# A constant moved into padding columns, warm-up products on fp32 data, and a new issue order, in a gated-linear-attention plus MLP-mixer kernel

## The chip, the cores and the metric

One core of one Trainium2 chip runs the kernel. The metric is the device time of one execution in microseconds (us). Matrix products run on TensorE (PE in the profile, its weight loads PEld), elementwise work on VectorE (DVE), ScalarE (ACT) and GpSimd (POOL), and DMAs are issued from SyncE (SP) and ACT.

## The reference

Inputs q, k, v and alpha have the shape 4 x 8 x 768 x 48 (batch, heads, steps, head dimension), in float32. A recurrent attention runs over the 768 steps, and its output x (4 x 768 x 384) goes through a mixer of two small MLPs:

```python
state = zeros((B, H, D, D))
for t in range(S):
    state = alpha[:, :, t, :, None] * state + einsum('bhd,bhe->bhde', k[:, :, t], v[:, :, t])
    y[:, :, t] = einsum('bhd,bhde->bhe', q[:, :, t], state)
...
xt = x.transpose(0, 2, 1)
h = maximum(xt @ w_tok1, 0) @ w_tok2          # 768 -> 256 -> 768
u = x + h.transpose(0, 2, 1)
out = u + maximum(u @ w_ch1, 0) @ w_ch2       # 384 -> 1536 -> 384
```

## The kernel before

The steps of a batch are cut into three chunks of 256, so there are twelve chunks, 0 to 11. In a chunk a partition holds two neighbouring steps ("slots"), and the first 64 partitions are one half (128 steps), the last 64 the other. The recurrence is replaced by products: with c the running sum of log(alpha) inside a half, queries are scaled by exp(c), keys by exp(-c), and the output is a masked product of the two plus a term with the state at the start of the half.

Names of operations carry their chunk at the end. For chunk n, `ld_at`, `ld_kt`, `ld_qt`, `ld_vt` load alpha, k, q, v. `ln` (chunks 0 to 2, the "wide" ones) or `P`, `ln1`, `lnP`, `r1` (the others) take logarithms into the tile `la`, which has 64 columns a head, 48 of data and 16 of padding. `cumw` or `cum` forms the running sums c in PSUM by products with a triangular matrix, and behind them 16 columns of sums over each half, one pair a head. One of each pair must vanish in exp for the partitions of the other head; for that a product of the identity with a small constant tile `off` adds -1024 there. `E`, `Et` and `IE` are the exps of c, of the sums and of -c. `kk`, `kl`, `qq`, `ql` scale keys and queries (`k0a`, `q0r` prepare the first slot), `vb` casts v, `vs` swaps halves of it. `trk` and `trq` transpose on TensorE and `evk`, `evq` copy the result out of PSUM (chunks 6 to 11 use the DMA transposes `dk`, `dq` and a copy `pq`). `G` is the product of keys and queries, `mask` its masking, `K` the product for the state, `s`, `sa`, `sm` the state's update, `i` and `y` the two terms of the output, `x` its copy to bf16.

For a mixer of batch b, `t1` and `t2` are the products with w_tok1 and w_tok2, `ht` the relu between them, `u` the residual add, `up` and `ut` (batches 0 and 1) or the DMA transposes `ux` the turning of u, `c1` the product with w_ch1, `rt` its relu, `c2` the product with w_ch2, `o` the residual add and `st` the store. `ldw` loads a piece of weights, `cw` casts it.

`f1` and `f3` are fillers: one or three products of zeros into a bank that an operation is about to overwrite, for TensorE alone; nobody reads them.

Each engine runs its instructions in order. That order is written out: the string `ORDER` lists all operations, each with a letter for its engine (t TensorE, s ACT, v DVE, g POOL, y SP), and the string `BUFS` names the buffers in the order in which they are first needed. The order between engines is kept by waits on data and buffers alone, with one addition: operations of DVE and POOL that read and write SBUF only (`shared`) wait for the last such operation of the other engine.

Of the kernel before, what the change touches and what calls it, by code (L numbers as in the profile page):

```python
# [102 lines left out]
OFF = -1024.0  # L103
NS, NM, NDT, NDC = 6, 3, 2, 12
# [12 lines left out]
def build(g):  # L117
# [12 lines left out]
    def attention(n):  # L130
# [19 lines left out]
        if n in WIDE:  # L150
            lnp = O("ln", act(800, True), 0, writes=[la], reads=[at], preds=[ld["at"]], emit=lambda e: g.lnw(la, at))
            cb = V("pair")
            cum = O("cumw", pe([384] * 4 + [4] * 8 + [16]), 2, writes=[cb, E, IE], reads=[la], preds=[lnp] + fill("cumw", cb),
# [4 lines left out]
        else:  # L158
# [7 lines left out]
            cum = O("cum", pe([384] + [4] * 4 + [16]), 2, writes=[cb, E, IE], reads=[la], preds=[lnp] + fill("cumw", cb),  # L166
# [10 lines left out]
        def scale(names, dst, src, f, pre, raw):  # L177
            return [O(nm, either(dve(384 * len(sl)), pool_tt(384 * len(sl))), 5, writes=[dst], reads=[src, f], port=True,
                      preds=(pre if 0 in sl else raw) + ([e2] if f is IE else [e1]),
                      emit=lambda e, sl=sl: g.scaled(e, dst, src, f, wide, sl)) for nm, sl in zip(names, slots)]  # L180
# [198 lines left out]
kk1v ld_vt1y vb1v K1t sm1_0v sa0_1t trk1t E2s ld_qt2y Et2s sm0_1v vs1_0g y1_0t evk1s ql2v sa1_1t qq2v x1_0s ib1t  # L379
sm1_1v y0_0t vs0_1s x0_0s G0_1t trq2t mask0_1v ld_kt2y kl2g f1_G11t G1_1t mask1_1v ia1t y0_1t kk2g trk2t ld_vt2y vb2s  # L380
K2t sa0_2t ldw_wt10y vs1_1g y1_1t ldw_wt11y evk2v evq2s G0_2t x0_1s f3_G12t G1_2t cw_wt11s cw_wt10g t1_0_1_0t sm0_2v
ib2t ia2t mask0_2v t1_0_1_1t vs0_2s y0_2t t1_0_0_0t t1_0_0_1t t1_0_1_2t mask1_2v x1_1s vs1_2g y1_2t x0_2v ldw_wt20y
t1_0_0_2t t1_0_0_3t t1_0_1_3t t1_0_1_4t t1_0_0_4t x1_2s t1_0_0_5t t1_0_1_5t ht_0_1s ht_0_0v cw_wt20g t2_0_2t ld_at3y
P3g t2_0_0t ldw_wt21y cw_wt21g u_0_2v ld_at4y P4g u_0_0v t2_0_1t lnP3s ln13s cum3t u_0_1v t2_0_3t u_0_3v t2_0_4t ln14s
r14s t2_0_5t IE3s lnP4s up_0_0t ut_0_0s up_0_1t ldw_wc11y cum4t IE4s u_0_4v u_0_5v up_0_2t ut_0_2s E4s ut_0_1v
cw_wc11g E3s c1_0_2_0t ldw_wc13y ld_kt3y cw_wc13g c1_0_6_0t c1_0_3_0t k0a3v kl3v kk3v kb3g c1_0_6_1t c1_0_3_1t
rt_0_3_1v rt_0_2_0v ldw_wc12y cw_wc12s r13s c1_0_2_1t c1_0_7_1t rt_0_3_0v ldw_wc15y cw_wc15s c1_0_7_0t rt_0_7_0v trk3t
c1_0_4_1t rt_0_6_0s ldw_wc10y c1_0_11_0t ka3s ldw_wc14y cw_wc14g rt_0_2_1s cw_wc10s rt_0_6_1v rt_0_4_1v ld_qt3y
c1_0_5_1t evk3s q0r3v ql3v c1_0_8_1t rt_0_11_0s qq3v ld_vt3y vb3v vs0_3v kc3v rt_0_5_1s c1_0_0_1t c1_0_8_0t rt_0_0_1s
rt_0_7_1s rt_0_8_1s c1_0_9_0t c1_0_1_0t vs1_3v rt_0_1_0s trq3t c1_0_5_0t rt_0_9_0v evq3s rt_0_8_0s c1_0_1_1t K3t  # L390
# [12 lines left out]
ld_qt7y u_1_0v lnP8s ln18s t2_1_1t u_1_1v t2_1_5t u_1_5v up_1_1t r17s c2_0_3_2t up_1_0t c2_0_3_3t u_1_4v up_1_2t
ld_qt8y dk6y ut_1_1v E7s o_0_3v ut_1_2v ut_1_0s k0a7g P10g vs0_6s kk7v ld_kt9y dk7y cum8t IE8s k0a8g c1_1_5_0t dq6y
ld_qt9y c1_1_9_0t o_0_0v P9g c1_1_8_0t q0r7v qq7g c1_1_10_0t c1_1_6_1t vs1_6s rt_1_5_0s r18s c1_1_4_0t kb6s E8s
c1_1_1_0t c1_1_7_1t rt_1_1_0v ka6s rt_1_9_0v c1_1_1_1t rt_1_4_0s c1_1_8_1t vs1_7s rt_1_8_0v kc6g c1_1_2_0t c1_1_11_1t
rt_1_11_1v vs0_7g rt_1_6_1s dq7y rt_1_1_1s rt_1_8_1v c1_1_7_0t c1_1_0_0t q0r8v rt_1_7_0s c1_1_3_1t rt_1_7_1s
rt_1_10_0s ld_vt8y K6t rt_1_2_0v ka7s kc7s c1_1_4_1t s0_6v sa1_6v ld_vt9y kk8g sm1_6g c1_1_5_1t rt_1_5_1s c1_1_3_0t
rt_1_3_0v c1_1_11_0t lnP9s rt_1_0_0s rt_1_3_1v pq6g c1_1_9_1t rt_1_11_0s kb7s c1_1_10_1t rt_1_10_1s rt_1_4_1v
rt_1_9_1v cum9t c1_1_0_1t k0a9g K7t sa0_7v rt_1_0_1v E9s IE9s sm0_7g sa1_7v c1_1_2_1t rt_1_2_1s c2_1_1_0t G1_6t qq8g  # L410
G0_6t mask0_6v ld_qt10y c2_1_3_0t c2_1_3_1t c2_1_3_2t c2_1_3_3t c1_1_6_0t c2_1_1_1t c2_1_4_0t dk8y kk9v ln110s pq7s
ln19s r110s r19s q0r9g sm1_7g mask1_6v dq8y rt_1_6_0s dk9y c2_1_1_2t G1_7t G0_7t o_1_3v ld_kt10y ib7t ib6t y1_6t vb8s
vs1_8s mask1_7v c2_1_4_1t c2_1_4_2t y0_6t c2_1_4_3t mask0_7v vs0_8s o_1_4v c2_1_1_3t o_1_1v lnP10s x1_6s kc8s K8t qq9g
dq9y sa0_8v ka9s vb9s cum10t c2_1_0_0t E10s ld_kt11y x0_6v ia7t y0_7t IE10s pq8g G0_8t mask0_8v ld_at11y vs1_9s G1_8t
# [481 lines left out]
```

## Time and profile before

| what | value |
|---|---|
| time, median of 3 runs | 163.1 us (163.03 to 163.98) |
| the profiled execution | 162.81 us, span 161.1 us |
| TensorE busy | 154.0 us, 96% of the span |
| VectorE / ScalarE / GpSimd busy | 117.2 / 101.1 / 64.4 us |
| DMA | 34.46 MB, mean 214 GB/s |

The span reaches from the first to the last instruction that the profiler saw; the execution's own time has 1.7 us more around it. In the rows, a line number is that of kernel.py, and as all products of the attention go through one helper, they share the line 607 and are told apart by their tiles: `ps<-zs` is a filler, `ps<-la,u` the running sums, `ps<-off,idn` the constant, `ps<-idn,pkk` a transpose of keys. A matmul's duration includes its way through the array, so neighbouring ones overlap, and x8 merges eight of them.

### The profile page before, as it was taken

The numbers are of one execution on the slowest core, as the hardware profiler recorded it, in microseconds if no ns is written. First come the engines' busy times: TensorE is split into PE (matmuls) and PEld (weight loads), VectorE is DVE, ScalarE is ACT, GpSimd is POOL, SyncE is SP. The second block draws the span as 40 slices with busy tenths as digits, with TensorE's granted clock in tenths as the row PEclk, the third lists the DMA queues.
The fourth block names the chain that finished last, engine by engine and source line by source line (L and its number), as shares of the span: only waits on it lengthen the run. The fifth ranks groups of instructions, "written<-read, shape, count | busy, mean of one in ns | idle before, by whom it ended". The sixth has DMA issues, their size and how long they took to land.

```text
span 161.1 us, 4038 instructions
## 1 busy us (share of the span) xinstructions
PE 154.0 (96%) x1598; PEld 98.7 (61%) x1598; DVE 117.2 (73%) x211; ACT 101.1 (63%) x190; POOL 64.4 (40%) x78
## 2 busy tenths in 40 slices
PE   7969898899999999999999999999999999999992
PEld 2556665666675666766666776666666566655661
DVE  4169796969899999858879999896696813654151
ACT  3794995999996867996999973889610002243000
POOL 4044396330915381976988994024320000000000
PEclk9987999999999999999999999999999999999999
DMA  4999999999999899999998999997110174331215
GB/s 121 323 325 311 296 336 347 353 283 271 293 368 285 202 300 288 316 224 265 235 250 168 190 304 173 166 263 212 54 49 4 26 169 146 140 108 49 98 58 187
DMA packets 76322, 34.46 MB, mean 214 GB/s; under 512 B 68112, under 2 KB 76304, under 8 KB 76304
## 3 DMA queue, kind: packets, MB, share of 16 engines
q1 hardware_dynamic: 74288, 31.66, 77.1%
q10 hardware_dynamic: 2016, 2.56, 4.4%
q8 instruction: 12, 0.20, 0.5%
q14 instruction: 6, 0.05, 0.1%
HBM read 25.17 MB, written 4.72 MB: 185 GB/s over the span
## 4 chain that ended last, share of the span: by engine, by line
PE 91%; ACT 5%; DVE 1%; issue 1%; DVEq 0%
PE ps L832 29%; PE ps L837 29%; PE ps L607 19%; PE ps L813 5%; PE ps L808 5%; PE ps L669 3%; ACT tpq L700 1%; ACT IE L640 1%; ACT E L640 1%; PE ps L824 1%; ACT tpk L700 1%; ACT ut L700 1%; DVE ht L805 0%; DVE ut L701 0%; ACT E L644 0%
## 5 line engine op out<-in xcount | busy, mean ns | idle before, releaser
L837 PE MATMUL ps<-wc,rt 128*128 128x384 bf16 (+2 forms) x300 | 52.4, 320 | 0.0
L832 PE MATMUL ps<-ut,wc 128*128 128x384 bf16 x288 | 50.9, 326 | 0.5 <-DVE ut L701 0.5
L803 ACT ACTIVATE rt<-ps 128x384 bf16<-128x384 f32 x56 | 26.1, 491 | 29.1 <-PE ps L832 26.1
L832 PEld LDWEIGHTS <-wc 128*128 128x128 bf16 x288 | 27.1, 98 | 17.5 <-issue 0.6
L837 PEld LDWEIGHTS <-rt 128*128 128x128 bf16 x300 | 27.4, 98 | 16.2
L723 DVE TENSOR_TENSOR gtm<-ps,mk 128x1024 bf16<-128x1024 f32 x24 | 28.7, 1218 | 2.6 <-PE ps L607 2.5
L805 DVE TENSOR_SCALAR rt<-ps 128x384 bf16<-128x384 f32 x40 | 20.6, 551 | 7.5 <-PE ps L832 7.4
L841 DVE TENSOR_TENSOR in<-ps,u 128x384 f32<-128x384 f32 (+2 forms) x25 | 13.1, 537 | 13.6 <-PE ps L837 13.2
L700 ACT CAST vb<-in 64x384 bf16<-64x384 f32 (+1 forms) x23 | 14.8, 649 | 2.1 <-DMA in<-in_v_dram 1.4
L656 POOL TENSOR_TENSOR pkq<-in,E 128x768 bf16<-128x768 f32 (+1 forms) x9 | 13.0, 1457 | 7.8 <-ACT IE L640 6.9
L817 DVE TENSOR_TENSOR u<-ps,x 128x384 bf16<-128x384 f32 x24 | 11.7, 550 | 1.3 <-PE ps L813 1.1
L774 POOL TENSOR_TENSOR ss<-tmp,E 128x384 bf16<-128x384 f32 x9 | 7.5, 836 | 7.8 <-DVE tmp L771 5.1
L656 POOL TENSOR_TENSOR pkk<-in,IE 128x384 bf16<-128x384 f32 (+1 forms) x6 | 8.4, 1409 | 5.4 <-ACT x L700 3.0
L808 PE MATMUL ps<-x,wt 128*128 128x384 bf16 x48 | 10.4, 325 | 0.0
L652 POOL TENSOR_TENSOR in<-in,lf 128x384 f32<-128x384 f32 x5 | 5.0, 1006 | 12.8 <-DVE rt L805 7.1
L592 POOL TENSOR_TENSOR in<-in 128x384 f32<-128x384 f32 x8 | 8.0, 1000 | 4.9 <-DVE pkk L656 3.7
L607 PE MATMUL ps<-tpq,tpk 48*64 48x128 bf16 (+1 forms) x288 | 8.6, 224 | 1.3 <-ACT E L644 0.9
L607 PE MATMUL ps<-zs 128*128 128x512 bf16 x25 | 8.5, 485 | 1.1 <-DVE zs L507 1.1
L813 PE MATMUL ps<-ht,wt 128*128 128x384 bf16 x48 | 8.6, 325 | 0.5 <-DVE ht L805 0.5
L700 ACT CAST x<-ps 128x384 bf16<-128x384 f32 x16 | 7.7, 481 | 2.2 <-PE ps L607 1.8
L607 PEld LDWEIGHTS <-tpk 48*64 48x64 bf16 (+1 forms) x288 | 6.1, 104 | 4.4 <-issue 2.6
L607 PE MATMUL ps<-vb,gtm 128*128 128x48 bf16 x192 | 8.7, 183 | 0.0
(93 smaller groups left out, 214.9 us busy)
## 6 DMA issues: line engine op xcount, KB each, us to landing
in<-in_alpha_dram SPq DMA_DIRECT2D x12, 384.0 KB, 5.3
in<-in_q_dram SPq DMA_DIRECT2D x12, 384.0 KB, 5.6
in<-in_k_dram SPq DMA_DIRECT2D x12, 384.0 KB, 5.0
in<-in_v_dram SPq DMA_DIRECT2D x12, 384.0 KB, 5.5
in<-in_moe_w_ch_dram SPq DMA_DIRECT2D x12, 384.0 KB, 6.2
out_dram<-in ACTq DMA_DIRECT2D x12, 192.0 KB, 2.0
out_dram<-in SPq DMA_DIRECT2D x11, 192.0 KB, 2.2
in<-in_moe_w_tok_dram SPq DMA_DIRECT2D x4, 384.0 KB, 5.7
```

The lines of the kernel that those rows point to most:

```text
L607: return self.pe.matmul(out, lhsT=lhsT, rhs=rhs, start=start, stop=stop, skip_group_check=True)
L656: self.shared(self.eng[e].tensor_tensor(self.t(dst)[:, c : c + z, :, 0:D], self.t(src)[:, :, c : c + z, :].rearrange("p h s d -> p s h d") ...
L700: return self.act.copy(d, s)
L723: self.nc.vector.tensor_tensor(self.t(gtm)[:, hf, :, :], self.pair(gp).rearrange("p a (j t) -> p (a j) t", t=128), bass.AP(tensor=m.tensor ...
L803: self.act.activation(d, s, AF.Relu)
L805: self.nc.vector.tensor_scalar_max(d, s, 0.0)
L808: self.pe.matmul(self.bank(bank)[:, 0:HD], lhsT=self.wt1[:, kc, m * 128 : m * 128 + 128], rhs=self.t(x), start=(kc == 0), stop=(kc == NS - 1))
L813: self.pe.matmul(self.bank(bank)[:, 0:HD], lhsT=self.wt2[:, kc, i * 128 : i * 128 + 128], rhs=self.t(hts[kc]), start=(kc == 0), stop=(kc = ...
L817: self.nc.vector.tensor_tensor(self.t(u)[:, i % 3], self.bank(bank)[:, 0:HD], self.t(x), ALU.add)
L832: self.pe.matmul(self.bank(bank)[:, 0:HD], lhsT=self.wc1[:, kc, mc * 128 : mc * 128 + 128], rhs=self.t(ut)[:, 3 * half : 3 * half + 3, kc, ...
L837: self.pe.matmul(self.bank(bank)[:, 0 : cz - ca], lhsT=self.t(rts[mc][0])[:, i * 128 : i * 128 + 128], rhs=self.wc2[:, mc, ca:cz], start=( ...
L841: self.nc.vector.tensor_tensor(self.row(o)[:, ca:cz], self.bank(bank)[:, 0 : cz - ca], self.t(u)[:, i % 3, ca:cz], ALU.add)
```

## The change

Three things are changed. The product with `off` is gone: -1024 stands in two padding columns of `la` (row 0 and row 64), and the running-sum product takes 50 columns a head in place of 48 and spreads it by the triangular matrix. So c and the sums lie together, 50 columns a head, in PSUM and (chunks 3 to 11) in the tile `E`, and what reads them takes that step. The fillers become one product each, on zeros read as fp32, of 384 columns for `f3` and 128 for `f1`, where they were three and one of 512 in bf16. And `ORDER` and `BUFS` are new as a whole; the set of operations is the same. Some stay on their engine and move in the order, some change the engine.

```diff
-        self.off = T([128, 16], BF16, "off")
-        self.zs = T([128, 128], BF16, "zs")
+        self.zs = T([128, 256], BF16, "zs")
...
-        off = self.off.rearrange("p (c r) -> p c r", r=2)
-        dv.memset(self.off, 0.0)
-        dv.memset(off[0:64, :, 1:2], OFF)
-        dv.memset(off[64:128, :, 0:1], OFF)
+        for t in self.T["la"]:
+            dv.memset(t[0:1, 0, :, D + 1 : D + 2], OFF)
+            dv.memset(t[64:65, 0, :, D : D + 1], OFF)
...
     def fill(self, bank, count):
-        for _ in range(count):
-            z = self.zs
-            z = bass.AP(tensor=z.tensor, offset=z.offset, ap=[list(z.ap[0]), [0, 4], [1, 128]])
-            self.mm(self.bank(bank), self.zs, z, True, True)
+        z, n = self.zs.bitcast(F32), 384 if count > 1 else 128
+        r = bass.AP(tensor=z.tensor, offset=z.offset, ap=[list(z.ap[0]), [0, n // 128], [1, 128]])
+        self.mm(self.bank(bank)[:, 0:n], z, r, True, True)
+
+    def heads(self, bank, w=D):
+        return bank[:, 0 : H * DT2].rearrange("p (h c) -> p h c", c=DT2)[:, :, 0:w]
+
+    def sums(self, b, a, slots):
+        t = b[:, 0 : H * DT2].rearrange("p (h c) -> p h c", c=DT2)
+        for j in range(4):
+            for sl in slots:
+                self.mm(t[:, 2 * j : 2 * j + 2, D:DT2], a[:, sl, 2 * j : 2 * j + 2, :], self.sel, False,
+                        j == 3 and sl == slots[-1])
...
     def cumw(self, cb, la):
         b0, b1, a = self.bank(cb, 0), self.bank(cb, 1), self.t(la)
-        self.mm(b1[:, 0:HD], self.u2, a[:, 0, :, 0:D], True, False)
-        self.mm(b1[:, 0:HD], self.u2, a[:, 1, :, 0:D], False, True)
-        self.mm(b0[:, 0:HD], self.u2, a[:, 0, :, 0:D], True, False)
-        self.mm(b0[:, 0:HD], self.us, a[:, 1, :, 0:D], False, True)
-        ...
-        self.mm(b1[:, HD : HD + 16], self.idn, self.off, False, True)
+        self.mm(b1[:, 0 : H * DT2], self.u2, a[:, 0, :, 0:DT2], True, False)
+        self.mm(self.heads(b1), self.u2, a[:, 1, :, 0:D], False, False)
+        self.mm(self.heads(b0), self.u2, a[:, 0, :, 0:D], True, False)
+        self.mm(self.heads(b0), self.us, a[:, 1, :, 0:D], False, True)
+        self.sums(b1, a, (0, 1))
```

The start of the new order, with the engines' letters (loads of SP in their own order are at0 at1 kt0 vt0 at2 qt0 qt1 kt1 qt2 vt1 kt2 vt2 wt10 wt11 wt20 at4 wt21 at3 wc10 wc11 wc13 wc12 wc14 kt3 qt3; before they were at0 at1 qt0 kt0 qt1 vt0 at2 kt1 vt1 qt2 kt2 vt2 wt10 wt11 wt20 at3 wt21 at4 wc11 wc13 kt3 ...):

```diff
-f1_trq0t f3_cumw0t ld_at0y ln0s ld_at1y f1_K0t f3_K0t f3_cumw1t f3_trq0t ln1s cumw0t Et0s f3_trk0t E0s ld_qt0y qq0v
-ql0v ld_kt0y cumw1t IE0s kl0v trq0t E1s IE1s kk0v ld_qt1y ql1g evq0s trk0t evk0v qq1g Et1s G0_0t mask0_0v G1_0t
-ld_vt0y vb0s K0t s0_0v f3_trq1t vs0_0g f1_trq1t trq1t ld_at2y ln2s evq1s sa1_0t ib0t mask1_0v ld_kt1y kl1g cumw2t IE2s
...
+f1_trq1t f3_cumw1t f3_K0t ld_at0y ln0s f3_trk0t ld_at1y ln1s f3_cumw0t cumw0t IE0s cumw1t E1s IE1s Et1s Et0s ld_kt0y
+f1_K0t ld_vt0y kl0v kk0v trk0t vb0v K0t vs1_0g s0_0v ld_at2y ln2s cumw2t evk0v ld_qt0y E0s qq0v ql0v IE2s ld_qt1y qq1v
+ql1v E2s f1_trq0t f3_trq0t trq0t evq0s Et2s sa1_0t sm1_0v f3_trq1t trq1t G0_0t evq1s ld_kt1y kl1v kk1v ld_qt2y ql2g
+qq2g trk1t evk1s ld_vt1y mask0_0v G1_0t mask1_0v vs0_0g f1_G11t G1_1t mask1_1v G0_1t vb1s ib0t y1_0t x1_0s K1t vs1_1s
+vs0_1s ld_kt2y kk2v sa0_1t sm0_1v ld_vt2y y0_0t x0_0s trq2t ia1t mask0_1v sa1_1t kl2g ib1t y1_1t trk2t evq2s x1_1s
+y0_1t x0_1s vb2g K2t vs0_2s sm1_1v sa0_2t ia2t evk2v G0_2t ... f3_G12t G1_2t ...
...
```

Later places that the prediction names, in the new order: the first products of batch 0's channel MLP with chunk 3 among them (TensorE: `c1_0_0_0 c1_0_3_0 c1_0_2_0 c1_0_1_0 c1_0_6_0 c1_0_7_1 c1_0_7_0 c1_0_3_1 c1_0_5_0 c1_0_6_1 c1_0_0_1 c1_0_1_1 c1_0_4_1 trk3 c1_0_5_1 c1_0_9_0 c1_0_2_1 trq3`), where DVE has `rt_0_7_1 k0a3 kk3 kl3 q0r3` and POOL then `ql3 qq3` (DVE had `q0r3 ql3 qq3` before); and the end, where the last stores `st_3_0h0` and `st_3_0h1` are issued by SP (ACT before).

More of the change, by code (lines that the diff above doesn't have):

```diff
@@ L103 @@
 OFF = -1024.0
+DT2 = D + 2
 NS, NM, NDT, NDC = 6, 3, 2, 12
@@ L179, in scale @@
                       preds=(pre if 0 in sl else raw) + ([e2] if f is IE else [e1]),
-                      emit=lambda e, sl=sl: g.scaled(e, dst, src, f, wide, sl)) for nm, sl in zip(names, slots)]
+                      emit=lambda e, sl=sl: g.scaled(e, dst, src, f, wide, sl, DT2 if f is E and not wide else D))
+                    for nm, sl in zip(names, slots)]
         kk = scale(("kk", "kl"), pkk, kt, IE, k_in, [ld["kt"]])
@@ L620, in cum @@
-        self.mm(b[:, HD : HD + 16], self.idn, self.off, False, True)
+        self.mm(b[:, 0 : H * DT2], self.u2, a[:, 0, :, 0:DT2], True, False)
+        self.sums(b, a, (0,))
     def cumw(self, cb, la):
         b0, b1, a = self.bank(cb, 0), self.bank(cb, 1), self.t(la)
-        self.mm(b1[:, 0:HD], self.u2, a[:, 0, :, 0:D], True, False)
-        self.mm(b1[:, 0:HD], self.u2, a[:, 1, :, 0:D], False, True)
-        self.mm(b0[:, 0:HD], self.u2, a[:, 0, :, 0:D], True, False)
-        self.mm(b0[:, 0:HD], self.us, a[:, 1, :, 0:D], False, True)
@@ L633, in expE @@
+        self.sums(b1, a, (0, 1))
     def expE(self, E, cb):
[L634 removed]
+        self.act.activation(self.t(E)[:, 0 : H * DT2], self.bank(cb)[:, 0 : H * DT2], AF.Exp)
     def expIE(self, IE, cb):
[L637 removed]
+        self.act.activation(self.t(IE)[:, 0:HD].rearrange("p (h d) -> p h d", h=H), self.heads(self.bank(cb)), AF.Exp,
+                            scale=-1.0)
@@ L652, in q0r, with scaled @@
         self.shared(self.eng[e].tensor_tensor(a, a, self.t(r1), ALU.mult))
-    def scaled(self, e, dst, src, f, wide, slots):
+    def scaled(self, e, dst, src, f, wide, slots, step):
         f, c, z = self.t(f), slots[0], len(slots)
@@ L658, in scaled @@
             bass.AP(tensor=f.tensor, offset=f.offset + (c * HD if wide else 0),
-                    ap=[list(f.ap[0]), [HD if wide else 0, z], [D, H], [1, D]]), ALU.mult))
+                    ap=[list(f.ap[0]), [HD if wide else 0, z], [step, H], [1, D]]), ALU.mult))
     def vcast(self, e, vb, vt):
@@ L754, in amul @@
     def amul(self, E, hf, wide):
-        f = self.t(E)[:, (2 * HD if wide else HD) + 2 * hf :]
-        return bass.AP(tensor=f.tensor, offset=f.offset, ap=[list(f.ap[0]), [4, 4], [1, 2], [0, D]])
+        at, step = (2 * HD + 2 * hf, 2) if wide else (DT2 * hf + D, DT2)
+        f = self.t(E)[:, at:]
+        return bass.AP(tensor=f.tensor, offset=f.offset, ap=[list(f.ap[0]), [2 * step, 4], [1, 2], [0, D]])
     def st(self, t):
```

143 lines of the change are left out of this document (67 added, 76 removed), and 22 rows, old and new, of the table BUFS.

## The prediction, made before the changed kernel ran

> **What bounds the kernel now.** I read the page first, then TensorE's waits, then the start by the microsecond, because the page says that TensorE is hardly ever idle.
>
> ```profile
> span 161.1 us, 4038 instructions
> PE 154.0 (96%) x1598; PEld 98.7 (61%) x1598; DVE 117.2 (73%) x211; ACT 101.1 (63%) x190; POOL 64.4 (40%) x78
> PE 91%; ACT 5%; DVE 1%; issue 1%; DVEq 0%
> PE ps L607 <- DVE zs L507: 1.1, 1, 1.1
> PE ps L607 <- ACT E L644: 0.9, 1, 0.9
> ```
>
> The third line is the chain that ended last: 91% of it is TensorE. The last two are the longest waits of TensorE (total, times, longest), and both lie in the first 11 us. And behind the start? The two windows below (us, length, then busy time of PE, PEld, DVE, ACT, POOL) stand for 40 to 155 us.
>
> ```profile
> 40.00:50.00 10.00, 10.00 (x124) 6.73 (x123) 9.10 (x14) 9.57 (x19) 5.72 (x7) 1.00 1.07 331
> 140.00:150.00 10.00, 10.00 (x64) 6.07 (x63) 5.41 (x12) 3.81 (x8) 0.00 (x0) 1.00 0.28 99
> ```
>
> From the first hidden-layer product (c1, line 832) on, no gap is left, and 64 products in 10 us is one every 0.156 us. This stretch can lose by a new order, by waits, but can win only what is taken off TensorE. So a better order pays only ahead of that product. That start is worth a walk:
>
> ```profile
> 1.06 4.59 PE L607 MATMUL ps<-zs 128*128 128x512 bf16 x14 [1.06 <-DVE zs L507]
> 1.46 0.15 PEld L607 LDWEIGHTS <-zs 128*128 128x128 bf16 x1 [0.28 <-issue]
> 4.27 0.84 ACT L601 ACTIVATE la<-in 128x768 bf16<-128x768 f32 x1 [2.18 <-DMA in<-in_alpha_dram]
> 5.48 0.65 PE L607 MATMUL ps<-la,u 128*128 128x384 bf16 x3
> 6.34 0.17 PE L607 MATMUL ps<-off,idn 128*128 128x16 bf16 x1
> 6.31 0.10 PEld L607 LDWEIGHTS <-idn 128*128 128x128 bf16 x1
> 6.36 0.81 PE L607 MATMUL ps<-zs 128*128 128x512 bf16 x3
> 6.63 0.81 ACT L640 ACTIVATE E<-ps 128x768 f32<-128x768 f32 x1
> 11.79 0.84 ACT L601 ACTIVATE la<-in 128x768 bf16<-128x768 f32 x1 [0.25 <-DMA in<-in_alpha_dram]
> 12.43 1.87 PE L607 MATMUL ps<-zs 128*128 128x512 bf16 x4
> 14.79 1.31 ACT L700 COPY tpq<-ps 128x1024 bf16<-128x1024 bf16 x1 [2.16 <-PE ps L669]
> ...
> 18.58 0.40 PE L607 MATMUL ps<-tpq,tpk 48*128 48x128 bf16 x8 [0.38 <-ACT tpk L700]
> 22.61 2.37 DVE L723 TENSOR_TENSOR gtm<-ps,mk 128x1024 bf16<-128x1024 f32 x2
> 27.04 1.14 PE L813 MATMUL ps<-ht,wt 128*128 128x384 bf16 x6 [0.49 <-DVE ht L805]
> 27.56 2.88 DVE L817 TENSOR_TENSOR u<-ps,x 128x384 bf16<-128x384 f32 x6 [0.58 <-PE ps L813]
> 31.33 0.97 PE L832 MATMUL ps<-ut,wc 128*128 128x384 bf16 x5 [0.49 <-DVE ut L701]
> ```
>
> Two things set it. Loads: alpha of chunk 0, the first load, is used at 4.27; alpha of chunk 2, the seventh, at 11.79: one load each 1.25 us. And the clock of TensorE, the column behind the busy times:
>
> ```profile
> 7.00:8.00 1.00, 1.00 (x14) 0.66 (x12) 0.54 (x2) 1.00 (x2) 0.00 (x0) 1.00 1.17 325
> 8.00:9.00 1.00, 0.48 (x9) 0.45 (x8) 1.00 (x4) 1.00 (x3) 0.00 (x0) 1.00 1.17 325
> 9.00:10.00 1.00, 0.81 (x11) 0.45 (x8) 0.51 (x2) 1.00 (x2) 0.33 (x1) 1.00 1.17 325
> 10.00:11.00 1.00, 0.18 (x5) 0.27 (x7) 0.61 (x1) 1.00 (x3) 1.00 (x2) 0.87 1.17 326
> 11.00:12.00 1.00, 1.00 (x26) 1.00 (x24) 0.53 (x1) 0.75 (x2) 0.63 (x1) 0.50 1.17 325
> 14.00:15.00 1.00, 1.00 (x15) 0.82 (x14) 1.00 (x3) 0.21 (x1) 0.22 (x1) 0.92 1.18 321
> ```
>
> It falls to 0.50 at about 10.74 (0.26 of that microsecond at half speed makes 0.87) and is back at about 14.16: 3.4 us of half clock, after 3.4 us (7.33 to 10.74) in which TensorE was busy some 1.9 us. In that stretch, four fillers took 1.7 us to the next product, 0.42 each (so 0.21 at full clock), and ACT's next copy waited 2.16 us behind them.
>
> **The change, part by part.** *The product with off.* Twelve go, one a chunk. Its start is 6.34, and the next matmul starts at 6.36: 0.02 us of TensorE. Its weight load, the row at 6.31, takes 0.10, which is the other end. I take 0.025, since loads are mostly pulled under other products: -0.3 us (-0.24 to -1.2). Against it, twelve products grow from 384 to 400 columns. Three of 384 stand in 0.65 us, of which the last one's own duration is 0.33: 0.16 each, so 16 columns are 0.007 us, +0.08. Net -0.2 us.
>
> *Strided tiles.* The sums now lie 48 of every 50 columns; exp, the scaling and the state products read with that step. No row shows that step. The nearest rows are the two transposes of the groups:
>
> ```profile
> L669 PE MATMUL ps<-idn,pkk 128*128 128x128 bf16 x48 | 4.0, 220 | 0.1
> L669 PE MATMUL ps<-idn,pkq 128*128 128x128 bf16 x48 | 3.7, 220 | 0.5 <-DVE pkq L656 0.5
> L607 PE MATMUL ps<-off,idn 128*128 128x16 bf16 x12 | 2.0, 169 | 0.0
> L700 ACT COPY tpk<-ps 128x1024 bf16<-128x1024 bf16 x3 | 3.0, 1014 | 0.0
> L723 DVE TENSOR_TENSOR gtm<-ps,mk 128x1024 bf16<-128x1024 f32 x24 | 28.7, 1218 | 2.6 <-PE ps L607 2.5
> L656 DVE TENSOR_TENSOR pkk<-in,IE 128x384 bf16<-128x384 f32 x7 | 3.6, 555 | 0.1
> L656 POOL TENSOR_TENSOR pkq<-in,E 128x384 bf16<-128x384 f32 x4 | 3.9, 1005 | 6.9 <-ACT IE L640 6.9
> L805 DVE TENSOR_SCALAR rt<-ps 128x384 bf16<-128x384 f32 x40 | 20.6, 551 | 7.5 <-PE ps L832 7.4
> ```
>
> Keys (pkk) are written as runs of 64 with gaps, queries in one run, and both take 220 ns. So zero; at worst a product doubles, 0.16 us on each of the three per wide chunk. The Trainium skill's page "SBUF — State Buffer", section "Door 1: The DMA port swizzle", says that any non-contiguous PSUM pattern significantly slows matmuls. The two rows do not agree with it at runs of 64; runs of 48 no row shows. By it this term would be a loss, which I keep as a rival.
>
> *Fillers.* A triple of 512 columns in bf16 becomes one product of 384 columns on fp32 data, a single becomes one of 128. No row has an fp32 product. In columns the new one is a quarter of the old; nearest below is therefore a quarter of the time (0.05 us for a single at full clock), and above, four passes with a weight load each uncovered. A filler's load took 0.15 us at half clock (the row at 1.46), so the first block of five products could grow by up to 20 x 0.15 = 3 us. I take the old duration, a pass of four, because 384 and 128 are exactly the old column counts over four; both ends stay. The Trainium skill's page "FP8 and Floating Point Precision", section "TensorE Precision Notes", says four passes; by it the sum is the same as mine. In old units, 13 stand ahead of the first sums now (1+3+3+3+3), 14 before.
>
> *Set-up.* Three memsets of off become four of la; the filler's own memset doubles (0.05 us). All but that end by 3.4 us, ahead of the 4.27 at which la is first written.
>
> *The order: start, at full clock.* Every step below is a start or an end on the clock of this trace. First sums (cumw0): 5.48, less one filler (0.21), plus the memset 0.05, is 5.3. Their first exp came 1.06 us behind the sums' start (6.54, the small one just ahead of the row at 6.63); now exp(-c) comes first, 6.4 to 7.2. DVE scales the two halves of the keys (0.5 each back to back) to 8.25, so TensorE transposes them (trk0) from 8.25; DVE casts v to 8.8, and TensorE's K0 runs to 9.6. Alpha of chunk 2 is the fifth load now: 4.27 + 4 x 1.25 = 9.3, ln to 10.1, sums 1.06 later, 11.2. exp(c) of chunk 0 stands behind that ln in ACT's queue: 10.95. DVE scales the queries to 11.9. Four fillers (0.85) stand ahead of trq0 on TensorE; they wait for bank 5, which DVE's copy evk0 empties at about 11.0, and end at 11.85, so they are hidden; trq0 ends at 12.5. ACT copies evq0 behind both exps of chunk 2 (12.7) to 14.0, evq1 to 15.2 and evk1 (1.01) to 16.1, without the gap of 2.16. So the second G of chunk 1 (G1_1) starts at 16.2; before it started at 18.58 (its row stands above). From there DVE is the queue that counts: mask of G1_1 to 17.9 (TensorE 0.4, mask 1.22), kk2 18.4, sm0_1 18.9, the other mask 20.0, sm1_1 20.5, evk2 21.1, then G of chunk 2 and its two masks, 21.6 to 24.0, which before began at 22.61 and ended at 24.98. y and ACT's x (0.5 each) 24.95, the last t1 25.3, ht behind one ln (0.5 each, hand-over) 25.95, t2 at 26.0. First u add 26.5, six of them 2.88, one ut copy 0.55: c1 starts at **30.0 against 31.33**, -1.3 us. Weights of c1 (the 19th load, 4.27 + 18 x 1.25 = 26.8, cast on POOL behind P4 and P3) are ready by 28.7. I leave some 0.1 to 0.3 us of hand-overs out.
>
> *The same with the half clock.* TensorE's work between 7.33 and 10.74 is now rest of the sums 0.2, trk0 0.6, K0 0.8, start of cumw2 0.6, one filler 0.2: 2.4 us at most, with waits of 0.85 and 0.6. That is near the 1.9 that went cold, far from the full windows that did not. So I expect 0.50 again from about 10.7. Then the rest of cumw2 costs 0.3 more, the four fillers ahead of trq0 0.85 more (0.42 each for 0.21), trq0 0.25 more: 1.4 us, and here they are in the chain, as evq0, evq1 and evk1 follow in ACT's queue. 30.0 + 1.4 = 31.4: nothing won. This is the likelier branch. The Trainium skill's page "TensorE: Matmul & The Clock Gate", Part 4, says that transposes do not count as busy for the gate; by that both windows are emptier still, and the branch likelier.
>
> *The rest.* By the letters of the order times these rows, POOL gets 5 us more, DVE 2.5 less, ACT 1 more; all have idle time for it. Two issues queue differently: the dk/dq transposes on SP stand among loads, as before, and the last stores go by SP instead of ACT:
>
> ```profile
> 157.67 0.62 DVE L841 TENSOR_TENSOR in<-ps,u 128x320 f32<-128x320 f32 x2 [0.66 <-PE ps L837]
> 158.19 0.82 ACTq L588 DMA_DIRECT2D out_dram<-in  x2
> ```
>
> TensorE's last pieces are the same (320 and 64 columns) in the same order, so the tail is 0, +-0.2.
>
> *Sum.* Profiled execution 162.81 us, span 161.1, 1.7 around it. 161.1 + 0.05 (start, half clock) - 0.2 = 160.95, plus 1.7: **162.6**. The median shown, 163.1, is 0.2% above its profiled run, less than a measurement tells; 1% is about what one can tell here, 1.6 us.
>
> **Rivals.** *The start stays at full clock*: -1.3 - 0.2 gives 161.3, and 160.9 if off cost its load. For it: where the 3.4 us windows fall decides. Against: the emptier stretch.
>
> *A new wait in chunk 3, slower than before*: the query's second and third scalings go to POOL (1.005 each, with a hand-over) in place of DVE (0.5). Behind c1's sixth product DVE does a relu, k0a, kk, kl and q0r (0.17 + 0.55 + 4 x 0.5), POOL 2.2: 7.9 us after c1's start if key and query have landed. TensorE reaches trq3 after 16 products of 0.49 and a transpose: 8.25. The margin is 0.35 us, and c1, evq3 and G3 queue behind trq3. It decides as soon as k0a3 starts over 0.35 us late: by a key (24th load) after about 35, or relus in arrears. A load two slots late (2.5 us) costs 2.1: 162.6 + 2.1 = 164.7. Against it: the 24th load by 1.25 us a slot is 33.
>
> *fp32 fillers cost weight loads, or are a quarter long and let the clock fall under the first sums*: 0.5 to 2.5 us in the start; 163.8. *The strided sums double*: 0.5 us in each of three chunks' sums, two in the chain: 163.6. *Order made no difference and the product was hidden anyway*: 162.8, inside the forecast.
>
> **How the numbers follow.** Forecast (162.0 to 163.4) 0.50; full clock 0.22; wait in chunk 3 or another of its kind 0.17; fillers 0.07; stride 0.04. 1% faster is below 161.5: most of the full-clock case, 0.16. 1% slower is above 164.7: somewhat over half of the wait and a fifth of the fillers, 0.11. Within: 0.73. Range 160.9 to 164.7.
>
> **What would show it.** TensorE's first sums at 5.3 and fillers of unchanged total (else the filler step is wrong); clock 0.50 somewhere from 10 to 16; trq0 at 12.5 or 14; c1's first product at 30.0 or 31.4; no wait of TensorE behind it; the off row gone. A wait over 0.5 us after 32 us, or half clock later than 16, would make it wrong.

## The result, and the profile after

The changed kernel takes 162.46 us (median of 11 runs, 161.54 to 164.09), the kernel before 163.1 us (11 runs, 162.49 to 164.26): a ratio of 0.9943, 95% interval 0.9918 to 0.9969. Repeated with 12 and 23 runs it was 0.9945, 0.9912 to 0.9978. So the change is worth 0.8 to 0.9 us, some 0.55%, with an interval from 0.2 to 0.9%. All runs of before that stood beside the experiments have a median of 163.25 us (87 runs).

The profiled execution after took 162.72 us. The page has (span; engines; chain that ended last):

```profile
span 161.0 us, 4005 instructions
PE 153.2 (95%) x1583; PEld 99.3 (62%) x1583; DVE 114.8 (71%) x208; ACT 101.7 (63%) x189; POOL 68.8 (43%) x83
PE 87%; DVE 5%; ACT 4%; issue 1%; POOL 0%; DVEq 0%
```

Span against span, almost nothing happened: 161.0 after 161.1. But inside there are two large moves of opposite sign. The first, from the timeline of after (start, duration, what, and in brackets the wait ahead of it):

```profile
4.32 0.84 ACT L601 ACTIVATE la<-in 128x768 bf16<-128x768 f32 x1 [2.23 <-DMA in<-in_alpha_dram]
5.66 0.66 PE L607 MATMUL ps<-la,u 128*128 128x400 bf16 x3
11.94 0.62 PE L675 MATMUL ps<-idn,pkq 128*128 128x128 bf16 x8
26.21 1.78 PE L820 MATMUL ps<-ht,wt 128*128 128x384 bf16 x10 [0.58 <-ACT ht L810]
26.73 2.88 DVE L824 TENSOR_TENSOR u<-ps,x 128x384 bf16<-128x384 f32 x6 [0.67 <-PE ps L820]
30.22 1.11 PE L839 MATMUL ps<-ut,wc 128*128 128x384 bf16 x4
```

c1 starts at 30.22 instead of 31.33: 1.11 us won in this pair of executions. The stretch that ran at 0.50 before now runs at 1.00; these are its windows (the clock is the column ahead of the DMA share, 1.17):

```profile
10.00:11.00 1.00, 0.89 (x13) 0.62 (x12) 1.00 (x3) 0.76 (x2) 0.21 (x1) 1.00 1.17 325
11.00:12.00 1.00, 1.00 (x10) 0.54 (x7) 1.00 (x3) 0.80 (x2) 0.00 (x0) 1.00 1.17 326
12.00:13.00 1.00, 1.00 (x12) 0.84 (x12) 1.00 (x3) 1.00 (x3) 0.00 (x0) 1.00 1.17 324
```

The second move lies behind 90 us, where before had no wait of TensorE at all. First the list of TensorE's waits (total, times, longest), then TensorE, then POOL and SP's queue from the timeline:

```profile
PE ps L607 <- DVE zs L508: 1.1, 1, 1.1
PE ps L607 <- POOL pkk L707: 1.1, 1, 1.1
PE ps L820 <- ACT ht L810: 0.6, 1, 0.6
...
94.25 0.34 PE L607 MATMUL ps<-vb,pkk 128*128 128x96 bf16 x4 [1.06 <-POOL pkk L707]
...
81.21 1.82 POOL L662 TENSOR_TENSOR pkk<-in,IE 128x768 bf16<-128x768 f32 x1
91.39 0.50 POOL L707 CAST vb<-in 64x384 bf16<-64x384 f32 x1
93.69 0.50 POOL L707 COPY pkk<-pkk 64x384 bf16<-64x384 bf16 x1 [1.81 <-ACT x L706]
...
86.86 2.66 SPq L686 DMA_TRANSPOSE tpk<-pkk  x1
```

The product K of chunk 9 waits for a copy on POOL (kc9) that overwrites part of the scaled keys. The keys were ready at 83.0 (81.21 + 1.82), POOL was free at 91.9, and the copy starts at 93.69: it must let the DMA transpose dk9 read the keys first. SP issued that at 86.86 and it landed 6.7 us later, at 93.6; no other of these transposes took as long. The profile names ACT as releaser; a second profile of the same kernel, under after_again below, names the DMA. TensorE lost 1.06 us there. From c1's start to the end of the span it is 129.8 us before (161.1 - 31.33) and 130.8 after (161.0 - 30.22): in this execution the stretch behind c1 lost about what the start won.

The rows of the other parts of the change, grouped by line and shape (count, busy time, mean ns):

```profile
L607 PE MATMUL ps<-zs 128*128 128x384 f32 x14 | 6.6, 604 | 0.0
L607 PE MATMUL ps<-zs 128*128 128x128 f32 x8 | 2.2, 365 | 1.1 <-DVE zs L508 1.1
L607 PE MATMUL ps<-la,u 128*128 128x400 bf16 x12 | 3.9, 332 | 0.5 <-ACT la L601 0.5
L607 PE MATMUL ps<-la,u 128*128 128x384 bf16 x6 | 1.5, 324 | 0.0
L675 PE MATMUL ps<-idn,pkk 128*128 128x128 bf16 x48 | 3.9, 220 | 0.4 <-DVE pkk L662 0.3
L607 PE MATMUL ps<-sel,la 128*128 128x4 bf16 x60 | 3.2, 164 | 0.0
```

An fp32 product leaves two records. The row of the constant is gone.

### The profile page after: what moved, and what is told of

Read it like the earlier page. It is cut to its first block, busy times and chain, and to the rows that moved or that the text cites. A ratio compares the mean times of both kernels' runs of the same rounds, so it can differ in the third digit from the quotient of the medians.

```text
span 161.0 us, 4005 instructions
## 1 busy us (share of the span) xinstructions
PE 153.2 (95%) x1583; PEld 99.3 (62%) x1583; DVE 114.8 (71%) x208; ACT 101.7 (63%) x189; POOL 68.8 (43%) x83
## 2 busy tenths in 40 slices
DMA packets 76322, 34.46 MB, mean 214 GB/s; under 512 B 68112, under 2 KB 76304, under 8 KB 76304
## 4 chain that ended last, share of the span: by engine, by line
PE 87%; DVE 5%; ACT 4%; issue 1%; POOL 0%; DVEq 0%
PE ps L839 29%; PE ps L844 29%; PE ps L607 18%; PE ps L815 5%; PE ps L820 4%; PE ps L675 2%; ACT tpq L706 1%; DVE u L824 1%; DVE pkq L662 1%; DVE pkk L662 1%; PE ps L831 1%; ACT tpk L706 1%; DVE wc L707 1%; ACT IE L646 1%; ACT E L646 1%
## 5 line engine op out<-in xcount | busy, mean ns | idle before, releaser
L810 ACT ACTIVATE rt<-ps 128x384 bf16<-128x384 f32 x51 | 23.2, 493 | 27.9 <-PE ps L839 25.2
L812 DVE TENSOR_SCALAR rt<-ps 128x384 bf16<-128x384 f32 x45 | 23.0, 552 | 12.1 <-PE ps L839 11.6
L662 POOL TENSOR_TENSOR pkq<-in,E 128x384 bf16<-128x384 f32 (+1 forms) x12 | 15.7, 1320 | 11.9 <-DVE in L658 5.7
L662 POOL TENSOR_TENSOR pkk<-in,IE 128x768 bf16<-128x768 f32 (+1 forms) x7 | 11.1, 1584 | 3.4 <-DVE pkk L662 1.5
L820 PE MATMUL ps<-ht,wt 128*128 128x384 bf16 x48 | 9.4, 325 | 0.6 <-ACT ht L810 0.6
L607 PE MATMUL ps<-zs 128*128 128x384 f32 (+1 forms) x22 | 8.5, 517 | 1.1 <-DVE zs L508 1.1
L662 DVE TENSOR_TENSOR pkk<-in,IE 128x384 bf16<-128x384 f32 (+1 forms) x10 | 6.1, 633 | 4.2 <-ACT IE L646 4.0
L707 POOL CAST vb<-in 64x384 bf16<-64x384 f32 (+1 forms) x10 | 5.6, 564 | 7.5 <-PE ps L607 7.0
L607 PE MATMUL ps<-tpq,tpk 48*64 48x128 bf16 (+1 forms) x288 | 8.1, 219 | 0.6 <-ACT tpk L706 0.4
L592 POOL TENSOR_TENSOR in<-in 128x384 f32<-128x384 f32 x7 | 7.0, 1000 | 3.5 <-DMA in<-in_alpha_dram 3.5
```

The costliest lines, as they stand in the source:

```text
L607: return self.pe.matmul(out, lhsT=lhsT, rhs=rhs, start=start, stop=stop, skip_group_check=True)
L662: self.shared(self.eng[e].tensor_tensor(self.t(dst)[:, c : c + z, :, 0:D], self.t(src)[:, :, c : c + z, :].rearrange("p h s d -> p s h d") ...
L810: self.act.activation(d, s, AF.Relu)
L812: self.nc.vector.tensor_scalar_max(d, s, 0.0)
L820: self.pe.matmul(self.bank(bank)[:, 0:HD], lhsT=self.wt2[:, kc, i * 128 : i * 128 + 128], rhs=self.t(hts[kc]), start=(kc == 0), stop=(kc = ...
```

## The experiments

**The three parts one at a time.** First the padding alone, in before's order and with its fillers:

```diff
-        self.mm(b1[:, HD : HD + 16], self.idn, self.off, False, True)
+        self.mm(b1[:, 0 : H * DT2], self.u2, a[:, 0, :, 0:DT2], True, False)
```

> The kernel before with the padding edit alone (order and fillers of before). Theory (the order's start makes the gain, the constant's product is small): 12 products fewer at 0.02 to 0.03 us each against 12 x 16 more columns, so 0.2 us less, ratio 0.998 to 1.000; c1 starts at 31.2 to 31.4, the clock falls to 0.50 from about 10.7 as before. Rival (each product cost its weight load too): 1 us less, ratio 0.993 to 0.995. Rival (strided sums are slow): the four products of cumw take more than 0.16 us each from start to start, ratio 1.003 or more.

Measured: 163.0 us, ratio 0.9967 (0.9937 to 0.9997). That lies between the theory's range and the rival's, and the interval (0.05 to 1.0 us) is too wide to choose. The profile is for the theory: the stretch from c1 to the end is 129.5 us against 129.8 before, -0.25 us for the nine products of that stretch, 0.028 each. c1 itself misses its date, 32.18 for 31.2 to 31.4, and the clock falls at 12.43, because the first sums begin late, at 6.32; counted from them, c1 comes after 25.86 us, as in before (25.85).

The fillers alone, in before's order:

```diff
-        for _ in range(count):
-            ...
-            self.mm(self.bank(bank), self.zs, z, True, True)
+        z, n = self.zs.bitcast(F32), 384 if count > 1 else 128
+        ...
+        self.mm(self.bank(bank)[:, 0:n], z, r, True, True)
```

> The kernel before with the fp32 fillers alone. Theory: a filler in fp32 lasts as long as the bf16 ones, so the first sums start at 5.5 to 5.9 and all behind is as before: the clock falls to 0.50 from about 10.7, c1 at 31.3 to 31.6, ratio 1.000 to 1.002. Rival (fp32 fillers, not the order, keep the clock up): no 0.50 between 10 and 15 us, the transpose of queries of chunk 1 at 13.3 in place of 14.1, c1 at 30.5, ratio 0.995.

Measured: 163.81 us, ratio 1.0026 (0.9998 to 1.0053): no gain, perhaps 0.4 us lost. The clock falls here too, at 11.74, and c1 comes at 32.21, 26.11 behind first sums that start at 6.10, later than expected.

The order alone (ORDER and BUFS of after, everything else of before):

> The kernel before with the new order alone (bf16 fillers, the product with off kept). Theory: the start keeps its gain, c1 at 30.2 to 30.6, the clock stays at 1.00, the wait of about 1 us ahead of K9 at 93 us is there too, ratio 0.994 to 0.998. Rival (fp32 fillers keep the clock up): 0.50 in a window between 9 and 16 us, c1 at 31 to 31.6, ratio 1.000 to 1.005.

Measured: 162.56 us, ratio 0.997 (0.9936 to 1.0005), in the theory's range. In its profile TensorE shows no half clock behind its first sums, as the theory had it. Two dates of the theory missed: c1 starts at 31.74, for its first sums start at 6.50 (25.24 from the one to the other, against 25.85 before), and there is no wait ahead of K9: 129.5 us from c1 to the end.

**The wait of K9.** Two loads that stand ahead of dk9 on SP go to ACT:

```diff
-ld_vt9y ... ld_kt10y
+ld_vt9s ... ld_kt10s
```

> The changed kernel with two loads (v of chunk 9, k of chunk 10) issued by ACT, so that SP reaches the DMA transposes dk9 and dq9 some 2 us earlier. Theory (the gain at the start is given back in the wait of K9 for kc9, and that for dk9's landing): no wait ahead of K9, dq9 early too, so the copy pq9 and G0_9 do not take its place; 1.0 us less than the changed kernel, ratio to before 0.986 to 0.990. Rival (something else is late next, or ACT's queue pays for the two issues): 0 to 0.3 us less, ratio 0.992 to 0.995.

Measured: 162.45 us, ratio 0.9956 (0.9928 to 0.9983), as after: the theory's 1.0 us did not come, the rival's case did. The wait at K9 is gone from the profile, and a wait of 0.7 us behind a transposed query (pq8, another DMA transpose) stands in its place; c1 to the end is 130.5 us.

With less load on the transfers:

```diff
+        if nm == "vt" and NB * b + k >= 6:
+            dst, src = dst[:, 0:4], src[:, 0:4]
```

> The kernel after, with the loads of v for chunks 6 to 11 cut to four of the eight heads (768 KB of the traffic is left out; the upper four heads of v are whatever the buffer held, so the output of those chunks is not the reference's; no instruction fewer). Theory D: the transfers, busy without a gap from 2 to 108 us, pace chunks 6 to 11, so the transposes of chunks 8 and 9 land earlier and the wait of K9 for kc9g (1.1 us) and those behind pq8 and pq9 go: the stretch from c1 to the end falls from 130.8 to 129.4-129.9 us, ratio .986 to .991. Rival S: the waits come from the order in SP's queue and the few buffers of the transposes, whatever the transfers' load: K9 still waits 0.7 us or more, stretch 130.4 to 131, ratio .993 to .996.

By the pages 1.18 MB were left out (33.28 for 34.46 MB), more than the 768 KB of the expectation. Measured: 162.55 us, ratio 0.9939 (0.9912 to 0.9965). c1 to the end fell to 129.6 us in its profile, as theory D had it, but the ratio is the one of theory S; and kernels with the full load (e5_10fill, e11_bf16fill) had 129.5 and 129.6 in their profiles too. So halving the loads of v in chunks 6 to 11 did not make the kernel faster, and the stretch of one profile proves nothing. It suggested that the wait belongs to an execution, which the next one asks.

> The kernel after, unchanged, with a second profile. Theory V (the wait of K9 belongs to one execution: in the profile of after the transpose of pkk of chunk 9 landed late; in three later kernels with the same order of SP and POOL there it didn't): no PE wait behind POOL L707 of over 0.3 us, the stretch from the first c1 product to the end is 129.4 to 129.9 us (130.8 before), time again .992 to .997 of before, and no execution with a mean granted clock below .993. Rival S (the order makes the wait): K9 waits 0.8 us or more again, stretch 130.4 to 131.

Measured: 162.44 us, ratio 0.9945 (0.9912 to 0.9978). The second profile of the kernel after, POOL first, then TensorE:

```profile
93.08 0.50 POOL L707 COPY pkk<-pkk 64x384 bf16<-64x384 bf16 x1 [0.71 <-DMA tpk<-pkk]
96.81 0.64 PE L607 MATMUL ps<-tpq,tpk 48*64 48x128 bf16 x32 [0.64 <-ACT tpq L706]
```

The wait of 1.06 at K9 did not come again, as theory V had it. But the copy did wait 0.71 us for the DMA transpose, by name, and one product later G of chunk 9 waited 0.64 us behind a transposed query. The stretch is 130.5 us (161.7 - 31.2), which theory S had and V had not. So each is half right. And the start of this second profile won next to nothing: c1 comes at 31.24, for 31.33 before, at full clock, mostly because the first sums start at 6.17 and the third wait 0.91 us for their alpha.

The loss sits at the DMA transposes of chunks 8 and 9: in two of two profiles of after and in e4_sp_relief, in none of e3, e5, e7, e8, e10, e11 or the two of e9 (e10 has a wait of 0.58 us for a copy of weights instead, at 48.2). It goes with the landing of these transposes: counted from c1, dq9 landed after 64.4 and 64.2 us in the two profiles of after and after 60.9 to 62.7 in those without the loss; in e4 it was dq8, 59.0 against 57.6 at most. What makes them land late in one execution and not in another stays open.

**Who keeps the clock up.** The six fillers behind the first sums taken out of after:

```diff
-f1_K0t ... f1_trq0t f3_trq0t ... f3_trq1t ... f1_G11t ... f3_G12t
```

> The kernel after without the six unread products that stand behind the first sums (before K0, trq0 twice, trq1, G1_1, G1_2); the ten at the very start stay. Theory F: it is the six that keep TensorE busy enough between 7 and 16 us; without them a window of half clock of about 3.4 us comes in, c1 starts 0.7 to 1.3 us later behind the first sums (25.2 to 25.9 instead of 24.5), mean granted clock .989 or less in most executions: ratio .998 to 1.003. Rival O: the new order alone keeps the full clock; the clock stays at .994 or more, and what the fillers took at full clock on TensorE beside its waits is won or lost by no more than 0.3 us: ratio .992 to .996.

Measured: 163.26 us, ratio 0.9965 (0.993 to 1.0); 8 of 12 executions with a mean granted clock below .993. For the clock that is theory F, the fillers are needed; the time lies between the two ranges. In its profile the clock falls later than expected, at about 17 us:

```profile
16.00:17.00 1.00, 0.27 (x8) 0.09 (x4) 1.00 (x2) 1.00 (x3) 1.00 (x2) 0.99 1.17 328
17.00:18.00 1.00, 0.89 (x16) 0.77 (x16) 1.00 (x2) 0.78 (x2) 0.94 (x2) 0.50 1.14 391
20.00:21.00 1.00, 1.00 (x22) 1.00 (x21) 0.87 (x2) 0.95 (x3) 1.00 (x2) 0.80 1.14 326
```

Down at 16.98, up at 20.40: 3.4 us again, and c1 starts at 32.0, 25.2 behind the first sums. Now the fillers as they were in before, but in the new order and with the padding:

> The kernel after with the fillers of before (bf16, one or three products of 512 columns) in place of the single fp32 ones; order and padding as in after. If the kind of filler decides nothing (two records of 0.64 us against three of 0.42 at half clock): ratio .992 to .997, no execution below .993 mean clock, within 0.3 us of after_again. If fp32 data costs what e2_fillers hinted (1.0026): .989 to .992, 0.4 us under after_again. If it is the fp32 data that keeps the clock up: some executions below .993, .996 or more.

Measured: 161.99 us, ratio 0.9921 (0.9891 to 0.9951), no execution of 12 below .993. So fp32 data is not what keeps the clock up, in the new order. With e2_fillers this is the second comparison in which fp32 fillers come out some 0.4 us dearer; neither is clear of its interval alone.

**The start.** One of the fillers ahead of the first sums left out:

```diff
-f1_trq1t f3_cumw1t f3_K0t ld_at0y ln0s f3_trk0t ...
+f1_trq1t f3_K0t ld_at0y ln0s f3_trk0t ...
```

> The kernel after with one of the filler products that stand ahead of the first decay sums left out (f3_cumw1, three bank writes; nothing of the result changes). Theory A: the first sums wait behind the fillers, not for their data, and the fillers end late when TensorE leaves half clock late; with 3 x 0.64 us less at half clock ahead of them the first sums start at 5.2 to 5.5 us (5.66 in the profile of after, 6.10 to 6.50 in the four other profiles), c1 at about 24.5 us behind them, and of those 0.3 to 0.5 us at the start at most 0.2 reach the end, because what is won at the start is given back in chunks 8 to 11: ratio to before .991 to .996. Rival B: nothing is given back and the whole start counts: .989 to .992. Rival C: the fillers left are too few, a window of half clock follows the first sums and c1 starts 1 us later: .999 to 1.003.

(It is one product, two records of 0.64 us at half clock, so 1.28 us and not 3 x 0.64.) Measured: 162.31 us, ratio 0.9942 (0.9909 to 0.9975), theory A's range but not by its reason: the profile has no loss in chunks 8 to 11. First sums at 5.36, as expected, but c1 at 30.7, 25.3 behind them and not 24.5: the third sums now wait 1.15 us for their alpha. In 2 of 12 executions the clock is below .993, at 163.43 us; the other ten have 162.05.

Both leftovers together:

> Two edits that each left something over, together: the loads of v of chunk 9 and k of chunk 10 issued by ACT instead of SP (e4_sp_relief), and one of the first fillers fewer (e5_10fill). Theory D (transfers set the pace behind c1): no better than either alone, ratio .992 to .996. Rival S (queue order sets it): the wait of K9 is gone and the start is 0.4 us earlier, both count: ratio .987 to .991.

> e9_both again, which stood on six runs of its own only. If its 161.57 us was luck of few runs: ratio .993 to .996, as after and e4 and e5 alone; if one filler fewer at the start and the two loads on ACT add up: .988 to .992, and under after_again of the same call by 0.4 to 0.8 us.

Measured: 161.57 us, ratio 0.9898 (0.9861 to 0.9935), and 161.47 us, ratio 0.9885 (0.9853 to 0.9917), six runs of its own each, none below .993. That is the range of rival S, and of the second expectation's second case; that the transfers alone set the pace behind c1 (theory D) is out. But it is more than a sum: alone, the two edits stood at 162.45 and 162.31, hardly under after's 162.46, and together they are worth 0.9 us. Why stays open. The twelve runs lie between 161.37 and 162.43, the 23 of after between 161.51 and 164.09: the best executions are alike, and the late ones are missing. It is the fastest version here, 0.6% under after. From its second profile:

```profile
span 159.6 us, 3999 instructions
5.07 0.66 PE L594 MATMUL ps<-la,u 128*128 128x400 bf16 x3
30.08 1.10 PE L826 MATMUL ps<-ut,wc 128*128 128x384 bf16 x4
```

c1 to the end is 129.5 us, with no wait at a DMA transpose.

One more filler fewer (the single f1_trq1):

> e9_both without the filler f1_trq1 at the start as well (two records of 128 columns, some 0.45 us each at half clock). If the fillers still hold the first sums in executions that leave half clock late: another 0.1 to 0.4 us under e9_again; if the sums now wait for ln (its end at 5.1 to 5.3 us) and the gap ahead of them keeps TensorE's clock low or drops it again later: 0.3 to 0.8 us over e9_again, with some executions below .993 mean clock.

Measured: 161.55 us, ratio 0.9886 (0.9851 to 0.992), the same as e9; no execution of 8 fell below .993, so neither case of the expectation came. Its profile is of the slowest of the eight executions, 162.65 us. There the sums start at 5.26, but at half clock (1.13 us for three products, 0.66 at full clock), which ends at 7.20 only:

```profile
5.26 1.13 PE L594 MATMUL ps<-la,u 128*128 128x400 bf16 x3
```

## Why the prediction came out as it did

The time came out 0.1 us from the forecast, and the range held it. The path to it did not hold at two steps, which cancelled in the profile; that the number was so near is luck.

**The half clock: the step that failed.** The prediction put TensorE's work between 7.33 and 10.74 at 2.4 us, "near the 1.9 that went cold", and judged the fall the likelier branch. The 2.4 was right, the reading of it wrong. Over all runs the mean granted clock is below .993 in 53 of 87 executions of before and in 17 of 24 with one part of the change in the old order (e1, e2), but in 2 of 103 in the new order with its six later fillers in place (both in e5). The profiled execution of before was one of the 53. e3 shows that the order does it; e8 that it needs the fillers.

Why the old stretch falls and the new one doesn't can be read from the windows themselves. The clock record of the traces gives the grid: every stretch between two changes is a whole multiple of 3.413 us (in e8, up at 6.74 and down at 16.98, three of them). Ahead of its first rise it holds nothing, and the column shows 1.00 there; that TensorE begins at half clock is seen in the fillers alone (in after a record each 0.64 us, later 0.32). Here are the 3.41 us ahead of a fall in before, in e1_padding, in e2_fillers and in e8_nofill, then stretches that stayed at 1.00: the one before that in e8 (3.41 earlier), one of after's start, and the last whole one of e8 (20.39 + 40 x 3.413 = 156.92). For each, the windows view of all engines, with TensorE first, and behind it that of the transposes alone (they have a line of their own, 669 in before; the one busy time is PE's; the last stretch has none):

```profile
7.33:10.74 3.41, 1.96 (x29) 1.45 (x27) 2.66 (x5) 3.41 (x7) 1.07 (x2) 1.00 1.17 325
7.33:10.74 3.41, 1.26 (x16) 1.00 1.17 325
...
9.02:12.43 3.41, 1.93 (x35) 1.52 (x37) 2.28 (x5) 3.41 (x6) 1.95 (x2) 1.00 1.17 322
9.02:12.43 3.41, 1.26 (x16) 1.00 1.17 322
...
8.33:11.74 3.41, 1.88 (x35) 1.48 (x34) 2.40 (x5) 3.39 (x6) 1.46 (x2) 1.00 1.17 322
8.33:11.74 3.41, 1.26 (x16) 1.00 1.17 322
...
13.57:16.98 3.41, 2.09 (x34) 1.44 (x32) 3.20 (x6) 3.41 (x6) 1.44 (x2) 1.00 1.17 326
13.57:16.98 3.41, 1.26 (x17) 1.00 1.17 326
...
10.16:13.57 3.41, 2.11 (x37) 1.61 (x37) 2.75 (x7) 2.98 (x7) 0.50 (x1) 1.00 1.17 325
10.16:13.57 3.41, 0.60 (x8) 1.00 1.17 325
...
8.01:11.42 3.41, 2.62 (x39) 2.04 (x40) 2.75 (x7) 2.98 (x7) 0.50 (x1) 1.00 1.17 325
8.01:11.42 3.41, 0.79 (x8) 1.00 1.17 325
...
156.92:160.33 3.41, 1.70 (x22) 1.23 (x20) 1.18 (x3) 0.00 (x0) 0.00 (x0) 1.00 0.82 287
```

By all of TensorE's busy time the fourth (2.09, fell) and the fifth (2.11, stayed) are the same, and the last has less (1.70) and stayed: the clock is at 1.00 to the end of the span. So do the last whole stretches of e5 and e9_again, with 1.74 each. Nor do weight loads (the second busy time) or counts part them, with 1.23 us and 22 products in the last one. Without transposes they part: 0.70, 0.67, 0.62 and 0.83 us of other work fell, 1.51, 1.83 and 1.70 stayed. (After's row starts 0.14 us late: the first rise is at 4.46, and in the stretch from 7.87 it is 2.48 less 0.79, or 1.69.) The Trainium skill's page "TensorE: Matmul & The Clock Gate", Part 4, says that transposes don't count as busy in the same way; these rows agree. How much a transpose counts they do not show. The prediction named that rule and drew the wrong conclusion: it called both windows emptier by it and the fall likelier, without taking the numbers off, 0.6 us of transposes in the new window and 1.26 in the old. By the rule, 1.8 would have stood against 0.7, and full clock would have been the forecast for the start. The old order packs trk0 and trq0 into one such stretch with gaps around them; the new one puts K0 and the third sums between them. Counted from the first sums, c1 comes after 25.85 to 26.11 us in the three profiles of the old order, all with the fall, and after 24.43 to 25.38 in the ten of the new order with all six later fillers.

What the half clock costs is seen within one kernel: before's executions below .993 have a median of 163.63 us, the others 162.85; e8's, of eight and four, 163.32 and 161.91.

**The chain of the start at full clock** held in the first profile: t2 at 26.21 for 26.0, the six residual adds from 26.73 in 2.88 us for 26.5 and 2.88, c1 at 30.22 for 30.0, trq0 ended at 12.56 for 12.5. **The first sums** were to start at 5.3 and started at 5.66. The step took 5.48 as a fixed date; it is not. ln ends at 5.16 (4.32 + 0.84), so the sums wait for fillers, and these end early or late with the moment at which TensorE leaves its first half clock. That moment differs between executions: in the two profiles of after the clock's first rise is at 4.46 and 5.50 and the sums start at 5.66 and 6.17; over all traces that record it, the rise lies between 3.92 and 7.20, and the sums start at up to 6.79. The Trainium skill's page "TensorE: Matmul & The Clock Gate", Part 1, section "What's actually happening", says that the window which decides runs freely; the rows agree, and the spread here is 0.5 us in one kernel.

**The wait behind the start** had its chance, 0.17, and a cost, 2.1 us, and was put in chunk 3 "or another of its kind". Chunk 3 showed none. One of another kind came, 1.06 us at K9, and by the prediction's own words a wait over 0.5 us after 32 us makes it wrong. It named the transposes' queue only to say that it stands among loads as before. But POOL's copy kc9 and the copies pq8 and pq9 on ACT stand behind those transposes, with little margin. That the earlier c1 uses it up is not shown: the second profile of after has c1 at 31.24 and the loss, e9_again has it at 30.08 and no loss. So the sum of the profile, -1.11 at the start and +1.0 behind, comes out as 161.0 where the forecast had 160.95 for other reasons.

**The product with off** was put at -0.2 net. The padding alone gave -0.25 us in the stretch of the profile and -0.25 us in the medians (163.0 for 163.25), though its ratio, 0.9967, would be 0.5. The rival's price was mis-summed: at a whole weight load each, -1.2 + 0.08 makes 162.81 - 1.3 - 1.1 = 160.4, not 160.9, so the low end of the range was set too high for it. **Strided tiles** at zero: 400 columns take 332 ns for 326 with 384, as the columns say, and 384 spread over 48 of every 50 take 324; the rival that the product doubles is out. The rule that the prediction weighed, of the Trainium skill's page "SBUF — State Buffer", section "Door 1: The DMA port swizzle", does not agree with these rows. **Fillers**: 8.8 us in total (6.6 + 2.2) where 8.5 stood, so the old duration was right, and both far ends, a quarter and 3 us more, are out; the clock didn't fall under them. **Engines**: POOL +4.4, DVE -2.4, ACT +0.6 us, for +5, -2.5 and +1.

**The whole, by medians:** 163.25 to 162.45 us. Half clock left out in 53 of 87 executions, at 0.78 us each (163.63 - 162.85), is 0.48; the product is 0.25; together 0.73 of 0.80, an estimate, since the two groups of executions may differ in more than the clock, and the 0.25 has the wide interval of e1. By it, that is why the time moved although the profiled pair didn't: one pair of executions holds one draw of the clock's phase and of the transposes each.

## What to carry to other kernels

A start that was won has to reach the end: look which transfers and copies have little margin behind it, and read the stretch from the last common milestone to the end by itself (129.8 against 130.8 us here). Where a clock falls in some executions only, one profile of each kernel can't show what an edit is worth; count the executions by their mean clock. And when a rule is used on a new stretch, use it first on the old one that it must explain.

## What the runs showed of the hardware

- An fp32 product shows as two records: for 384 columns 0.64 us apart at half clock, 1.28 us a product, as long as three bf16 products of 512 columns at 0.42.
- TensorE's clock fell after stretches of 3.41 us in which it was busy 55 to 61% of the time (1.88 to 2.09 us), 1.26 us of that with transposes. It stayed up after one of 62% with fewer (2.11, of it 0.60), and after three of 50 to 51% with none (1.70, 1.74, 1.74). At the ends of e7, e9_both and e11 it fell after 0.84 to 0.98 us with none.
- TensorE's clock changes on a grid of 3.413 us that does not start with the program: the first rise lay between 3.92 and 7.20 us in the traces here.
- The same program's first sums start 0.5 us apart in two executions, and its runs spread by 2.5 us (161.51 to 164.09); with one filler fewer ahead of them and two loads on another queue the spread is 1.1 us.
